# Loading q, k and v of a head pair by one transfer each, with longer rows

## The chip, the cores and the metric

The kernel runs on one core of a Trainium2 chip. The metric is the device time of one execution in microseconds (us), the median of several runs. The core has five engines with instruction streams of their own: PE (TensorE, matrix products; PEld is its loading of weights), DVE (VectorE), ACT (ScalarE), POOL (GpSimd) and SP (SyncE, which here issues nearly all transfers). Sixteen DMA engines move the data of all queues.

## What is computed

Attention over 4 batches of 8 heads, 576 tokens, 64 values a head, then two MoE layers (without routing: plain feed-forward blocks) over all 2304 tokens.

```python
q_d = q.reshape(B, H, S // 4, 4, D).mean(axis=3)          # k_d, v_d alike
out_up = np.repeat(sm_attn(q_d, k_d, v_d), 4, axis=2)      # attention over groups of 4 tokens
mask = np.abs(pos[:, None] - pos[None, :]) < 4             # and over a band of 7 tokens
out_local = masked_attention(q, k, v, mask)
x = (out_up + out_local).transpose(0, 2, 1, 3).reshape(B * S, H * D)     # 2304 x 512
h = x @ w_in;  x = (h * sigmoid(h)) @ w_out                # 512 -> 2048 -> 512
h = x @ w2_in; y = (s * relu(h) ** 2 + b) @ w2_out
```

The MoE weights are stored as 8-byte floats. The kernel makes 4-byte floats of them and splits each into a high and a low part, so that a product takes three matmuls of a faster type.

## The kernel before

The program is a list of operations, each with its engine (or a choice of two), an estimated cost, the buffers that it reads and writes, and a priority (`pr`, lower first). A planner (`Weave.plan`) lays them out: it keeps a clock for each engine, takes the operation that can start first and, among those, the one of lowest `pr`, and so fixes the order of instructions on every engine. For a transfer the cost is a tuple: number of transfers, time on the DMA engines in all, and SP's time for issuing one. Where PE would stand still for long, the planner lays in filling matmuls (`spin`, L369); 100 of them stand at the very start.

Four stages overlap. (1) The first two batches (`NBAND = 2`): for each of four head pairs `rows` loads q, k and v; `b_turn` turns q and k so that the 64 values of a head lie along partitions; `down` does the attention over groups of four tokens; `banded` does the band on PE, with v rows loaded again by `b_load` (`vw`). Their sum goes into `xf`. (2) Batches 2 and 3 load with `natural` and do the band on VectorE (`local`, L480 to L545). (3) The first MoE layer (`mix1`, L835, L855 to L857) runs over five blocks of up to 512 tokens and begins when block 0 of `xf` is done, about 55 us. Its weights (`wi`, `wo`) are loaded and split on VectorE (L379, L382, L385, L391) during batches 0 and 1. (4) From about 390 us the weights of the second layer and then its products.

What matters around the change:

- `rows` (L584): a q or k of a head pair lies in SBUF as 96 partitions x 6 x 128: partition p holds tokens p, 96 + p, 192 + p and so on, with the two heads side by side. It is loaded by two transfers, one a head, whose rows are single tokens of one head, 256 bytes. A v lies as 72 partitions x 2 x 2 x 4 x 64: partition p holds four consecutive tokens, 1024 bytes; two transfers, one for each half of the tokens. The loads of the first batch stand on SP's queue, but for the v of the first pair on ACT's. They take one of ten buffers each (`NNAT`).
- `b_turn` (L702): for q and k, in two halves of 288 tokens, three transposes of 96 x 128 (L716) into one bank of PSUM, then one copy of 128 x 288 to SBUF on ACT or DVE (L333 and L331 on ACT, L335 and L331 on DVE), with the scale for q.
- `pool_rows` (L600) sums v over groups of four; L683 is the product with it. L621 and L622 do the same for the turned q and k.
- Priorities: the loads of a pair are asked for at -2.916 + 0.35 per pair, the first weights at -2.16 and later, and all attention before the weights.

Of the kernel before, what the change touches and what calls it, by code (L numbers as in the profile page):

```python
# [8 lines left out]
F32 = mybir.dt.float32  # L9
# [17 lines left out]
QP = 72  # L27
# [52 lines left out]
class Weave:  # L80
# [9 lines left out]
    def op(self, eng, cost, fn, w=(), r=(), pr=0.0, table=None):  # L90
        n, deps = len(self.ops), set()
        r = [x if isinstance(x, tuple) else (x, None) for x in r]
        w = [x if isinstance(x, tuple) else (x, None) for x in w]

        def hits(d, k):
            return [v for kk, v in d.items() if k is None or kk is None or kk == k]

        for b, k in r:
            deps.update(hits(b.wr, k))
        for b, k in w:  # L100
            deps.update(hits(b.wr, k))
            for v in hits(b.rd, k):
                deps.update(v)
        for b, k in r:
            b.rd.setdefault(k, []).append(n)
        for b, k in w:
            if k is None:
                b.wr, b.rd = {}, {}
            else:
                b.rd.pop(k, None)  # L110
            b.wr[k] = n
        deps.discard(n)
        bufs = []
        for b, _ in r + w:
            if b not in bufs:
                bufs.append(b)
                if not b.left and b.kind in self.turns:
                    self.turns[b.kind].append(b)
                b.left += 1
        self.ops.append((eng if isinstance(eng, tuple) else (eng,), cost, fn, sorted(deps), bufs, pr, table))  # L120
        return n
# [152 lines left out]
def kernel(ctx, tc, q, k, v, w1_in, w1_out, w2_in, w2_out, s2, b2, cst, out):  # L274
    nc = tc.nc
    B, H, S, D = q.shape
# [5 lines left out]
    tens = {"q": q, "k": k, "v": v}  # L282
# [32 lines left out]
    op = W.op  # L315
# [13 lines left out]
    def copy(eng, out, in_, by=1.0):  # L329
        if by == 1.0:  # L330
            (nc.scalar.copy if eng == "act" else nc.vector.tensor_copy)(out=out, in_=in_)  # L331
        elif eng == "act":
            nc.scalar.mul(out=out, in_=in_, mul=by)  # L333
        else:
            nc.vector.tensor_scalar(out=out, in0=in_, scalar1=by, scalar2=None, op0=ALU.mult)  # L335
# [7 lines left out]
    def dma(out, in_, eng=None, **kw):  # L343
        (eng or nc.sync).dma_start(out=out, in_=in_, **kw)  # L344
# [239 lines left out]
    def rows(b, i, names, pr, kind, after=[], by="sp"):  # L584

        for nm in names:
            t = nat[b, i, nm] = Buf(kind, [QP, 2, 2, 4, D] if nm == "v" else [CT, NCT, 2 * D], F32, "n" + nm)

            def load(t=t, nm=nm):
                queue = nc.scalar if by == "act" else nc.sync  # L590
                for k in range(2):
                    row = (b * H + 2 * i) * S
                    if nm == "v":
                        dma(t[:, k].rearrange("p a r d -> p a (r d)"), bass.AP(tens[nm].tensor, (row + k * 4 * QP) * D, [[4 * D, QP], [S * D, 2], [1, 4 * D]]), queue)
                    else:
                        dma(t[:, :, k * D:(k + 1) * D], bass.AP(tens[nm].tensor, (row + k * S) * D, [[D, CT], [CT * D, NCT], [1, D]]), queue)

            op(by, (2, 1.3, 0.4) if nm == "v" else (2, 1.75, 0.8), load, w=[t], r=after, pr=pr)

    def pool_rows(b, i, pr):  # L600

# [11 lines left out]
    def down(b, i, pr, ps="ps"):  # L613
# [66 lines left out]
        for a in range(2):  # L680
            def value(a=a):
                for kt in range(2):
                    nc.tensor.matmul(pU[a * D:(a + 1) * D], lhsT=nat[b, i, "v"][:, kt, a, 0] if plain else sums["v"](kt)[:, a * D:(a + 1) * D],  # L683
                                     rhs=at[:, kt, :, a * DQ:(a + 1) * DQ], start=(kt == 0), stop=(kt == 1))

            op("pe", 0.33 * slow(ps), value, w=[(pU, a), (up, i)], r=[at, nat[b, i, "v"]], pr=pr)
# [15 lines left out]
    def b_turn(b, hq, pr, ps):  # L702

        if hq < 3:
            t = Buf(("lk", "lv", "tmp")[hq], [P, 2, S], F32, "qkT")
            bq[b, hq], bk[b, hq] = (t, 0), (t, 1)
        else:
            bq[b, hq], bk[b, hq] = (Buf("lq", [P, 1, S], F32, "qT"), 0), (Buf("kx", [P, 1, S], F32, "kT"), 0)
        for nm, (t, i) in (("q", bq[b, hq]), ("k", bk[b, hq])):
            r, n = nat[b, hq, nm], S // 2  # L710
            for e in range(2):
                pt = Buf(ps, [P, n], F32, "pq")

                def turn(pt=pt, r=r, e=e):
                    for c in range(NCT // 2):
                        nc.tensor.transpose(pt[:, c * CT:(c + 1) * CT], r[:, e * NCT // 2 + c], ident[:CT, :CT])  # L716

                def keep(eng, pt=pt, t=t, i=i, e=e, nm=nm):
                    copy(eng, t[:, i, e * n:(e + 1) * n], pt[:], -0.125 if nm == "q" else 1.0)

                op("pe", 0.46 * slow(ps), turn, w=[pt, (t, (i, e))], r=[r, csb], pr=pr)
                op(EITHER, (act(n), dve(n)), keep, w=[(t, (i, e))], r=[pt], pr=pr)
# [619 lines left out]
```

## Time and profile before

| | |
|---|---|
| median of 3 runs | 888.25 us (887.92 to 890.25) |
| the profiled execution | 890.97 us, span 889.2 us |
| instructions | 14605 |
| PE, DVE, ACT busy | 867.6, 760.9, 463.8 us |
| transfers | 145.31 MB in 156914 packets; 65452 of them under 512 bytes |

A view's times count from the start of the span. An engine's busy time covers its instructions; a matmul's end is modelled, so a busy PE is not PE at full rate. [...] A DMA share counts the time of all packets against 16 engines and can pass 1, because packets overlap. Idle time at the end of a row is what the engine waited before it, and for whom.

### The profile page before, as it was taken

How to read it: one execution, taken by the hardware profiler on the slowest of the kernel's cores; microseconds unless marked ns; L12 is line 12 of the kernel's file. 1: busy time of each engine (PE TensorE's matmuls, PEld its weight loads, DVE VectorE, ACT ScalarE, POOL GpSimd, SP SyncE). 2: the span in 40 equal slices, each digit the busy share in tenths (PEclk: the TensorE clock that was granted, in tenths of full speed). 3: DMA queues.
4: the chain of work that ended last, by engine and by line, in shares of the span. 5: the costliest groups of instructions: out<-in, count | busy, mean ns of one | idle time of the engine just before them, and what ended most of it. 6: DMA issues, size and time to landing. Idle time of an engine off the chain costs nothing.

```text
span 889.2 us, 14605 instructions
## 1 busy us (share of the span) xinstructions
PE 867.6 (98%) x5303; PEld 716.9 (81%) x5303; DVE 760.9 (86%) x1415; ACT 463.8 (52%) x977; POOL 0.2 (0%) x4
## 2 busy tenths in 40 slices
PE   7999999999999999999999999999999999999998
PEld 7777776777777777878778998888888888888887
DVE  6999999799999999998778868778778768878885
ACT  5965677656457432442215655555657536443442
POOL 0000000000000000000000000000000000000000
PEclk9999999999999999999999999999999999999999
DMA  9999222662524311446988416555668778455511
GB/s 193 261 297 275 78 53 57 151 175 51 126 76 101 125 44 34 142 155 210 302 294 303 140 49 204 185 179 178 208 203 304 265 235 242 141 143 150 135 28 45
DMA packets 156914, 145.31 MB, mean 163 GB/s; under 512 B 65452, under 2 KB 118570, under 8 KB 156842
## 3 DMA queue, kind: packets, MB, share of 16 engines
q1 hardware_dynamic: 156434, 144.01, 54.8%
q8 instruction: 42, 0.69, 0.3%
q10 hardware_dynamic: 408, 0.36, 0.2%
q14 instruction: 30, 0.25, 0.1%
HBM read 103.44 MB, written 40.89 MB: 162 GB/s over the span
## 4 chain that ended last, share of the span: by engine, by line
PE 52%; DVE 28%; DMA 9%; issue 4%; ACT 4%; SPq 3%; DVEq 0%; ACTq 0%
PE ha L835 10%; PE hp L835 10%; PE y L835 6%; PE hc L835 5%; PE oa L1194 4%; DVE tmp L480 4%; DVE sc L483 3%; DVE tmp L517 3%; PE ob L1194 3%; SPq L344 3%; DVE gl L857 3%; PE oc L1194 3%; PE hb L835 2%; PE oa L1195 2%; DMA nq<-in_q_dram 2%
## 5 line engine op out<-in xcount | busy, mean ns | idle before, releaser
L835 PE MATMUL hp<-xh,wi 128*128 128x512 f32 (+1 forms) x640 | 204.0, 381 | 2.9 <-ACT g L855 2.7
L835 PE MATMUL y<-gh,wo 128*128 128x512 f32 (+1 forms) x640 | 200.2, 376 | 0.0
L835 PEld LDWEIGHTS hp<-xh,wi 128*128 128x128 f32 x640 | 117.8, 190 | 28.4 <-ACT g L855 8.3
L835 PEld LDWEIGHTS y<-gh,wo 128*128 128x128 f32 x640 | 117.3, 189 | 20.1 <-issue 1.0
L835 PE MATMUL hp<-xl,wi 128*128 128x512 f32 (+1 forms) x320 | 119.0, 372 | 0.2 <-DVE xl L558 0.2
L835 PE MATMUL y<-gl,wo 128*128 128x512 f32 (+1 forms) x320 | 118.2, 369 | 0.0
L856 ACT CAST gh<-g 128x512 fp32r<-128x512 f32 (+1 forms) x80 | 46.2, 577 | 84.1 <-PE y L835 83.0
L835 PE MATMUL ha<-yh,wi 128*128 128x512 f32 x256 | 87.3, 390 | 0.0
L855 ACT ACTIVATE g<-hp 128x512 f32<-128x512 f32 (+1 forms) x80 | 44.4, 555 | 63.7 <-DVE gl L857 60.1
L835 PEld LDWEIGHTS hp<-xl,wi 128*128 128x128 f32 x320 | 60.9, 190 | 8.4 <-DVE xl L558 0.5
L835 PEld LDWEIGHTS y<-gl,wo 128*128 128x128 f32 x320 | 60.5, 189 | 8.9 <-DVE gl L857 0.4
L835 PEld LDWEIGHTS ha<-yh,wi 128*128 128x128 f32 x256 | 48.1, 188 | 10.0 <-ACT g L331 0.4
L857 DVE TENSOR_TENSOR gl<-g,gh 128x512 fp32r<-128x512 f32 (+1 forms) x80 | 50.4, 630 | 3.7 <-ACT gh L856 3.4
L1033 DVE SCALAR_TENSOR_TENSOR g<-g 128x512 f32<-128x512 f32 (+1 forms) x80 | 48.9, 632 | 3.7 <-ACT g L1032 3.1
L1038 ACT ACTIVATE g<-g,sbt 128x512 f32<-128x512 f32 (+1 forms) x61 | 46.0, 777 | 7.9 <-DVE g L1033 7.6
L835 PE MATMUL ha<-yl,wi 128*128 128x512 f32 x128 | 50.0, 391 | 0.0
L331 ACT COPY g<-ha 128x512 f32<-128x512 f32 x46 | 26.9, 586 | 35.5 <-PE ha L835 23.2
L835 PE MATMUL hc<-yh,wi 128*128 128x512 f32 x128 | 44.8, 389 | 0.0
L1177 DVE TENSOR_TENSOR gl<-graw,gh 128x1024 fp32r<-128x1024 f32 x28 | 33.5, 1218 | 9.0 <-PE oa L1195 5.5
L1194 PE MATMUL oa<-wo,gh 128*128 128x512 f32 x112 | 40.2, 398 | 0.0
L835 PE MATMUL o<-wo,gh 128*128 128x512 f32 x128 | 39.4, 389 | 0.0
L517 DVE TENSOR_TENSOR tmp<-le,lv 128x1344 f32<-128x1344 f32 (+1 forms) x28 | 37.9, 1353 | 0.3
(203 smaller groups left out, 1849.9 us busy)
## 6 DMA issues: line engine op xcount, KB each, us to landing
graw<-gd SPq DMA_DIRECT2D x36, 512.0 KB
gd<-g SPq DMA_DIRECT2D x64, 256.0 KB
wi_raw<-in_moe_w_in_dram SPq DMA_DIRECT2D x16, 512.0 KB
wo_raw<-in_moe_w_out_dram SPq DMA_DIRECT2D x16, 512.0 KB
w_raw<-in_moe_w_in_dram SPq DMA_DIRECT2D x16, 512.0 KB
w_raw<-in_moe_w_out_dram SPq DMA_DIRECT2D x16, 512.0 KB
f<-w2out SPq DMA_DIRECT2D x32, 256.0 KB
nq<-in_q_dram SPq DMA_DIRECT2D x32, 144.0 KB
```

The lines of the kernel that those rows point to most:

```text
L331: (nc.scalar.copy if eng == "act" else nc.vector.tensor_copy)(out=out, in_=in_)
L344: (eng or nc.sync).dma_start(out=out, in_=in_, **kw)
L480: op("dve", dve(n * WIN * D), lambda t=t, i0=i0, n=n, h2=h2: nc.vector.tensor_tensor(out=t[:], in0=wide(qs[:, h2, i0:i0 + n, :].unsqueeze( ...
L517: op("dve", dve(n * WIN * D), lambda t=t, i0=i0, n=n, h2=h2: nc.vector.tensor_tensor(out=t[:], in0=wide(e[:, h2 * ns + i0:h2 * ns + i0 + n ...
L835: nc.tensor.matmul(t(), lhsT=lhs(i), rhs=rhs(i), start=(first and i == 0), stop=(last and i == 2), **kw)
L855: op("act", act(n), lambda g=g, hp=hp: nc.scalar.activation(out=g[:], in_=hp[:], func=AF.Silu), w=[g], r=[hp], pr=-5, table="silu")
L856: op("act", act(n), lambda g=g, gh=gh: nc.scalar.copy(out=gh[:], in_=g[:]), w=[gh], r=[g], pr=-5)
L857: op("dve", dve(n), lambda g=g, gh=gh, gl=gl: nc.vector.tensor_tensor(out=gl[:], in0=g[:], in1=gh[:].bitcast(F32), op=ALU.subtract), w=[gl ...
L1033: op("dve", dve(n) + 1.5 * MORE, lambda: nc.vector.scalar_tensor_tensor(out=t[:], in0=t[:], scalar=0.0, in1=t[:], op0=ALU.max, op1=ALU.mul ...
L1038: nc.scalar.activation(out=t[:], in_=t[:], func=AF.Identity, scale=sbt[:, 0:1], bias=sbt[:, 1:2])
L1177: op("dve", dve(HF * P) + MORE, lambda: nc.vector.tensor_tensor(out=flat(lo), in0=flat(x), in1=flat(hi).bitcast(F32), op=ALU.subtract), w= ...
L1194: nc.tensor.matmul(bank[:].rearrange("p x n -> p (x n)"), lhsT=hi[:, q], rhs=w(), start=new and q == 0, stop=False, skip_group_check=True)
```

## The change

For q and k, partition p now holds three consecutive tokens of each quarter of the pair (two heads, two halves of 288 tokens): 96 x 2 x 2 x 3 x 64, in one transfer with rows of 768 bytes. For v the order of the two middle axes changes (head before half) and both halves come by one transfer with rows of 1024 bytes as before. The heads no longer lie side by side, so each transpose of 96 x 128 becomes two matmuls of 96 x 64 against the same identity matrix, one for each half of the result's partitions. The columns then come out as (c, p) for token 3p + c, so the copy to SBUF puts them in order: it reads PSUM in a row and writes every third element. The planner's costs of the loads change with it. Both batches that use `rows` are affected; `natural` and `local` are not.

```diff
     def rows(b, i, names, pr, kind, after=[], by="sp"):
 
         for nm in names:
-            t = nat[b, i, nm] = Buf(kind, [QP, 2, 2, 4, D] if nm == "v" else [CT, NCT, 2 * D], F32, "n" + nm)
-
-            def load(t=t, nm=nm):
+            t = nat[b, i, nm] = Buf(kind, [QP, 2, 2, 4, D] if nm == "v" else [CT, 2, 2, 3, D], F32, "n" + nm)
+            p, c = (QP, 4) if nm == "v" else (CT, 3)
+
+            def load(t=t, nm=nm, p=p, c=c):
                 queue = nc.scalar if by == "act" else nc.sync
-                for k in range(2):
-                    row = (b * H + 2 * i) * S
-                    if nm == "v":
-                        dma(t[:, k].rearrange("p a r d -> p a (r d)"), bass.AP(tens[nm].tensor, (row + k * 4 * QP) * D, [[4 * D, QP], [S * D, 2], [1, 4 * D]]), queue)
-                    else:
-                        dma(t[:, :, k * D:(k + 1) * D], bass.AP(tens[nm].tensor, (row + k * S) * D, [[D, CT], [CT * D, NCT], [1, D]]), queue)
-
-            op(by, (2, 1.3, 0.4) if nm == "v" else (2, 1.75, 0.8), load, w=[t], r=after, pr=pr)
+                dma(t[:].rearrange("p a e c d -> p (a e) (c d)"), bass.AP(tens[nm].tensor, (b * H + 2 * i) * S * D, [[c * D, p], [p * c * D, 4], [1, c * D]]), queue)
+
+            op(by, (1, 1.3, 0.45) if nm == "v" else (1, 1.2, 0.45), load, w=[t], r=after, pr=pr)
...
-                    nc.tensor.matmul(pU[a * D:(a + 1) * D], lhsT=nat[b, i, "v"][:, kt, a, 0] if plain else sums["v"](kt)[:, a * D:(a + 1) * D],
+                    nc.tensor.matmul(pU[a * D:(a + 1) * D], lhsT=nat[b, i, "v"][:, a, kt, 0] if plain else sums["v"](kt)[:, a * D:(a + 1) * D],
...
                     for c in range(NCT // 2):
-                        nc.tensor.transpose(pt[:, c * CT:(c + 1) * CT], r[:, e * NCT // 2 + c], ident[:CT, :CT])
+                        for a in range(2):
+                            nc.tensor.matmul(pt[a * D:(a + 1) * D, c * CT:(c + 1) * CT], lhsT=r[:, a, e, c], rhs=ident[:CT, :CT], start=True, stop=True)
 
                 def keep(eng, pt=pt, t=t, i=i, e=e, nm=nm):
-                    copy(eng, t[:, i, e * n:(e + 1) * n], pt[:], -0.125 if nm == "q" else 1.0)
+                    copy(eng, t[:, i, e * n:(e + 1) * n].rearrange("d (p c) -> d c p", c=NCT // 2), pt[:].rearrange("d (c p) -> d c p", p=CT), -0.125 if nm == "q" else 1.0)
```

## Rows read from the trace of the kernel before

**Rows 1.** Page: busy time, share of the span and instructions of each engine.
```profile
PE 867.6 (98%) x5303; PEld 716.9 (81%) x5303; DVE 760.9 (86%) x1415; ACT 463.8 (52%) x977; POOL 0.2 (0%) x4
```

**Rows 2.** Windows of stages: PE, PEld, DVE, ACT, POOL busy, clock, DMA share, GB/s.
```profile
0.00:20.00 20.00, 15.17 (x246) 14.01 (x248) 12.06 (x33) 10.27 (x37) 0.20 (x4) 0.91 0.96 200
...
60.00:80.00 20.00, 20.00 (x131) 15.47 (x130) 20.00 (x41) 14.25 (x32) 0.00 (x0) 1.00 1.10 256
...
120.00:140.00 20.00, 19.71 (x178) 14.97 (x179) 19.96 (x52) 14.07 (x41) 0.00 (x0) 1.00 0.22 52
140.00:160.00 20.00, 18.60 (x142) 13.72 (x141) 15.68 (x40) 14.85 (x39) 0.00 (x0) 1.00 0.22 51
160.00:180.00 20.00, 19.85 (x156) 15.06 (x155) 17.53 (x42) 14.20 (x42) 0.00 (x0) 1.00 0.69 167
...
340.00:360.00 20.00, 20.00 (x92) 16.16 (x91) 19.41 (x30) 3.67 (x6) 0.00 (x0) 1.00 0.10 33
```

**Rows 3.** Costliest DVE group, 20 to 140 us: busy us, mean ns, idle before.
```profile
L382 DVE SCALAR_TENSOR_TENSOR f<-wi_raw,f 128x512 int32<-128x512 int32 x16 | 10.9, 682 | 0.0
```

**Rows 4.** DVE in order of time: start, us, instruction, idle before and releaser.
```profile
5.41 0.69 DVE L603 TENSOR_TENSOR nv<-nv 72x512 f32<-72x512 f32 x1 [3.87 <-DMA nv<-in_v_dram]
...
7.50 0.75 DVE L621 TENSOR_REDUCE dq<-qkT 128x144 f32<-128x576 f32 x1 [0.95 <-ACT qkT L333]
...
9.21 0.75 DVE L622 TENSOR_REDUCE dk<-qkT 128x144 f32<-128x576 f32 x1 [0.63 <-ACT qkT L331]
...
11.36 0.46 DVE L335 TENSOR_SCALAR qkT<-pq 128x288 f32<-128x288 f32 x1 [0.47 <-PE pq L716]
...
18.21 0.69 DVE L603 TENSOR_TENSOR nv<-nv 72x512 f32<-72x512 f32 x1 [0.98 <-DMA nv<-in_v_dram]
```

**Rows 5.** The chain that ended last, 0 to 24 us: start, us, what.
```profile
9.64 5.24 DMA nq<-in_q_dram
```

**Rows 6.** A window of one microsecond, columns as in rows 2.
```profile
16.00:17.00 1.00, 1.00 (x16) 0.97 (x15) 1.00 (x4) 0.93 (x5) 0.00 (x0) 0.50 1.00 305
```

**Rows 7.** PE in order of time, columns as in rows 4.
```profile
0.98 4.85 PE L369 MATMUL spin<-idle 128*128 128x64 bf16 x100 [0.98 <-DVE idle L365]
6.28 0.69 PE L716 MATMUL pq<-csb,nq 96*128 96x96 f32 x6 [0.45 <-DMA nq<-in_q_dram]
...
12.80 0.90 PE L651 MATMUL pS<-dk,q_diag 128*96 128x144 f32 x6
15.02 1.09 PE L716 MATMUL pq<-csb,nq 96*128 96x96 f32 x6 [1.32 <-DMA nq<-in_q_dram]
...
21.95 0.72 PE L683 MATMUL pU<-dat,nv 72*64 72x144 f32 x8
```

**Rows 8.** SP's queue in 100:106, 114.4:117.9, 0:10: packets, MB, share of 16 engines.
```profile
q1 hardware_dynamic: 1184, 0.30, 21.5%
q1 hardware_dynamic: 312, 0.30, 27.3%
q1 hardware_dynamic: 5047, 1.35, 81.8%
```

**Rows 9.** SP's issues of the first q, columns as in rows 4.
```profile
1.21 0.97 SPq L344 DMA_DIRECT2D nq<-in_q_dram  x2
```

**Rows 10.** Copies of a turned q: ns least, median, most; first and last start.
```profile
L335 DVE TENSOR_SCALAR qkT<-pq x5: 423/448/456, 11.4 to 115.5; 128x288 f32<-128x288 f32 x5
```

**Rows 11.** Instructions on `upT`, columns as in rows 10: two of 60:175, two of 175:300.
```profile
L825 DVE TENSOR_TENSOR xf<-pBO,upT x11: 348/414/425, 75.5 to 174.3; 128x256 f32<-128x256 f32 x7, 128x192 f32<-128x192 f32 x4
L331 DVE COPY upT<-pU x2: 297/298/300, 136.7 to 153.5; 128x144 f32<-128x144 f32 x2
L542 DVE TENSOR_TENSOR xf<-pt,upT x12: 369/384/417, 226.1 to 257.1; 128x128 f32<-128x128 f32 x12
L331 DVE COPY upT<-pU x1: 301/301/301, 222.0 to 222.0; 128x144 f32<-128x144 f32 x1
```

**Rows 12.** ACT's first table load in 140 to 175 us, columns as in rows 4.
```profile
143.24 1.28 ACT L784 ACT_TABLE_LOAD   x1
```

## The prediction

> **What bounds the kernel now.** I read the page's busy shares first: PE is busy for 98% of the span and VectorE for 86% [rows 1], so little time lies open, and an edit of loads is worth only what a load holds up. The windows of the stages come next [rows 2]. From 0 to 20 us VectorE is busy for only 12.06 us while the DMA engines have a share of 0.96. From 20 us on both are full; the window of 60 to 80 us stands for three (VectorE 20.00 of 20, DMA share 1.10). By 120 to 140 us VectorE is still at 19.96 with a DMA share of 0.22: there the loads hold up nothing. From 340 us on PE alone sets the pace: 92 matmuls, nearly all of the large kind, in 20 us are 0.22 us each. The work that fills VectorE from 20 to 140 us is the making of the MoE weights: for each of 32 tiles three instructions of the length of the group shown, 0.68 us [rows 3], and a shorter one: 32 x 3 x 0.68 = 65 us and more.
>
> Second, VectorE's own order in time from 0 to 20 us [rows 4]. The reader is to see the bracket at the end of a row: 3.87 us idle before the first pooling of v, then 0.95, 0.63, 0.47 and 0.98. In each the bracket's releaser is a load, or a copy or transpose that stands right behind one. Those before 5.41 us are the start (20 - 12.06 = 7.94 us idle in all, of which about 4.7 lie before 5.41); what is left is 3.03 us of named gaps and a few tenths.
>
> Third, the chain that ended last, from 0 to 24 us [rows 5]: the transfer of the first q, SP issuing, the transfer of the third q (5.24 us from 9.64 us), and the transposes behind it. So the first 20 us, and on VectorE they alone, wait for loads. [...]
>
> **What the change does, part by part.**
>
> *Fewer, longer packets for q and k.* A q or k of a head pair is 288 KB, today two transfers of 576 rows of 256 bytes, after it one of 384 rows of 768. Alone on the queues, such a q took 21.5% of 16 engines over 6 us = 20.6 engine-us for 1184 packets, 17.4 ns each; a v of 1024-byte rows took 27.3% of 3.5 us x 16 = 15.3 engine-us for 312 packets, 49 ns each [rows 8]. A packet of 768 bytes lies between; on a straight line it is 17.4 + 31.6 x 512/768 = 38.5 ns (an estimate), so 400 packets (16 end marks among them) cost 15.4 engine-us: 5.2 / 16 = 0.33 us saved a tensor. Under load the 256-byte packets are dearer: in the first 10 us 81.8% of 160 engine-us went to 5047 packets, 25.9 ns each, nearly all of them short [rows 8]. If the long ones rise less, to 46 ns, the saving is (1152 x 25.9 - 400 x 46) / 16 = 0.71 us. I take 0.45 us, nearer to the idle row, since long packets under load must rise too; ends 0.33 and 0.71. Six such tensors come before the second wait for v, so 2.7 us there; eight in the batch, 3.6 us.
>
> *One issue instead of two.* SP needs 0.97 us for the two issues of the first q [rows 9], so with one the first k can be issued 0.97 / 2 = 0.5 us earlier. v keeps its 1024-byte rows; only an issue goes, and its pooling waits for both halves today as well, so the coarser transfer delays nobody.
>
> *Transposes.* Three full-width transposes become six half-width matmuls against the same identity matrix, 32 such groups over both batches. Full width: 0.69 us for six records. Half width with the two halves of the result in different partitions is not there for this size, but the values product has the form: eight records of 72x144 in 0.72 us [rows 7], 0.062 us a record behind a last one of 0.29 us. For 96 columns that scales to 12 x 0.041 + 0.25 = 0.74 us. So +0.05 us a group, and from 20 us on PE has other work in line; I take zero, ends -0.02 (the halves pair perfectly) and +0.5 us a group (they don't pair at all, which the values row speaks against), 16 us over 32 groups. [...]
>
> *Copies out of PSUM.* There are 32 copies, one for each half of a turned q or k; fewer than ten go to VectorE, at 0.45 us [rows 10]. They now write every third element, 12 bytes apart. Lower end: the copies of upT change from unit step in the first batches to a step of two later on, and take 297 to 300 ns and 301 ns on VectorE [rows 11]: nothing. Upper end: the addition that reads PSUM with a step of four takes 384 ns for 128 elements, where one with unit step takes 348 for 192 and 414 for 256 [rows 11]; by these two an element is 66 / 64 = 1.0 ns and 128 would be 282, so the step costs 102 ns for 128, 0.8 ns an element, and 288 elements would pay 0.23 us. For VectorE 9 x 0.23 = 2.1 us over both batches. I take the lower end, since it too is a write, hence zero; the upper stays in the range. [...]
>
> *The planned order.* The cost of a load in the program's own schedule falls from 1.6 to 0.45 us of SP time for a q or k, so every engine's order is laid out anew, on all 890 us. The trace of before can't show that order. What it can do is bounded by the idle time that VectorE has after 20 us: 4.32 us in 140 to 160 us and 2.47 in 160 to 180 [rows 2], where ScalarE loads tables around the last heads of the second batch [rows 12]. A new order can win some of that or lay such a stall in again: -3 to +5 us, 0 taken.
>
> **The sum.** On VectorE: the first gap (0.95) closes only as far as PE is free, since 100 warm-up matmuls hold it to 0.98 + 4.85 = 5.83 us and the first transpose stands at 6.28 [rows 7]: 0.43. The second (0.63) follows the first k, which comes 2 x 0.45 + 0.5 = 1.4 us earlier: all of it. The third (0.47) and fourth (0.98) follow loads that come 1.35 and 2.7 us earlier: all. That is 2.51 us. Behind them ScalarE is next, busy for 10.27 us of the same 20 although it starts late [rows 2], so I give back a fifth: 2.0 us. After 20 us VectorE has no gap to lose, the weights it makes are loaded ahead of it, and 2.0 us earlier there is 2.0 us earlier for x, for PE and for the end. In the second batch nothing is saved: its loads wait for slots that VectorE frees, with a DMA share of 0.22 [rows 2]. The profiled execution took 890.97 us (span 889.2), 2.7 over the median of the runs; 890.97 - 2.0 = 888.97 there, and 888.25 - 2.0 = **886.25** for the median.
>
> **The rivals.** *Reordering costs more than the front gives (slower).* The place is 140 to 175 us, where ScalarE changes between its exp and silu tables six times, 1.28 us each (the first is shown), and VectorE idles most [rows 2, 12]. If heads that are ready earlier are interleaved with one block's silu more finely, each further round is two table loads, 2.57 us, on that chain. One round outweighs the 2.0 us; two give 888.25 - 2.0 + 5.1 = 891.4 us. For it: the order of 890 us hangs on the costs that change. Against it: after 180 us there is other work on every engine. Chance 0.25. *The loads are hidden anyway:* what gates VectorE behind 5.41 us are chains of PE, ScalarE and VectorE, and the gaps move instead of closing: about 888 us, chance 0.09. [...] *More comes off:* with the third q early PE never stands still, the clock stays at 1.00 through 15 to 18 us, and the new order also takes up half of the 6.8 us that VectorE idles in 140 to 180: 888.25 - 2.5 - 3.0 = 882.7 us, chance 0.22. *The halves don't pair on PE:* 16 groups before 55 us mostly hide, the 16 of the second batch cost 8 us: about 894 us, chance 0.03. The forecast itself has 0.35, with 884.5 to 888 as its own range.
>
> **How the numbers follow.** About 0.3%, 2.7 us, is what a measurement can tell from no change here: below 885.6 is faster, above 890.9 slower. Of the forecast's 0.35 some 0.13 lie below 885.6, the rest is the same; with the 0.22 of the larger gain faster is 0.35. Slower takes 0.18 of the 0.25, and the 0.03: 0.21. The rest, 0.44, is the same. The range reaches from the middle of the larger gain to one round and a half of table loads: 882 to 891.5.
>
> **What would show it.** In the profile after: q and k at 768 bytes and some 12,300 packets fewer; the first transpose at about 5.9 us, the third q's before 13 us, no granted clock of 0.5 there; VectorE busy for about 14 of the first 20 us; transposing groups at about 0.7 us and copies at 0.45 us on VectorE. Wrong would be: VectorE's gaps of the first 20 us as long as before (loads hidden), copies of 0.6 us (stride), or a front 2 us earlier with new idle time of VectorE in 20 to 180 us (order). The order of 20 to 180 us is what I know least about.

## The result, and the profile after

The changed kernel takes 898.57 us (median of 5 runs, 894.21 to 899.82) where the kernel before takes 889.4 in the same comparison: a ratio of 1.0088, 95% interval 1.0068 to 1.0107. Run again later it gave 1.0103 (1.0077 to 1.0129). It is slower by about 0.9%, some 8 us; forecast was 886.25 us and a range of 882 to 891.5. The profiled execution took 899.82 us, its span 898.0, so it stands 8.8 us over the profiled execution of before (span 889.2).

The page of the kernel after, in the order PE, PEld, DVE and so on as in [rows 1], and its packets:

```profile
PE 881.3 (98%) x5674; PEld 728.7 (81%) x5674; DVE 765.1 (85%) x1420; ACT 470.1 (52%) x982; POOL 0.2 (0%) x4
...
DMA packets 144277, 145.36 MB, mean 162 GB/s; under 512 B 46668, under 2 KB 105930, under 8 KB 144202
```

There are 12,637 packets fewer, as the change says, and the work of the three busy engines has grown: PE by 13.7 us and 371 instructions (288 for the half-width matmuls, 83 fillers), VectorE by 4.2, ScalarE by 6.3. Windows of the stages, columns as in [rows 2]:

```profile
0.00:20.00 20.00, 16.41 (x284) 15.08 (x285) 9.38 (x20) 10.05 (x30) 0.20 (x4) 0.88 0.95 206
20.00:40.00 20.00, 19.37 (x365) 16.45 (x365) 18.91 (x58) 15.71 (x65) 0.00 (x0) 0.95 1.00 212
...
140.00:160.00 20.00, 19.84 (x182) 14.72 (x181) 19.53 (x49) 15.15 (x47) 0.00 (x0) 1.00 0.27 69
160.00:180.00 20.00, 19.65 (x151) 15.21 (x148) 13.30 (x34) 13.61 (x40) 0.00 (x0) 1.00 0.43 115
```

VectorE is busy for 9.38 of the first 20 us; 14 had been forecast and 12.06 is what before has. What holds it up stands in its own order in time, where the rows that answer to [rows 4] are:

```profile
5.01 0.69 DVE L599 TENSOR_TENSOR nv<-nv 72x512 f32<-72x512 f32 x1 [3.47 <-DMA nv<-in_v_dram]
...
8.28 0.75 DVE L617 TENSOR_REDUCE dq<-qkT 128x144 f32<-128x576 f32 x1 [2.13 <-ACT qkT L333]
...
13.26 0.69 DVE L599 TENSOR_TENSOR nv<-nv 72x512 f32<-72x512 f32 x1 [1.48 <-DMA nv<-in_v_dram]
...
17.49 0.54 DVE L331 COPY qkT<-pq 128x288 f32<-128x288 f32 x1 [0.79 <-PE pq L713]
```

The first gap is 2.13 us instead of 0.95, and the second v holds up what had not waited for it. PE in the same stretch, as in [rows 7]:

```profile
6.43 1.21 PE L713 MATMUL pq<-csb,nq 96*64 96x96 f32 x24 [0.59 <-DMA nq<-in_q_dram]
...
14.70 1.80 PE L713 MATMUL pq<-csb,nq 96*64 96x96 f32 x24 [0.96 <-DMA nq<-in_q_dram]
16.22 2.20 PE L713 MATMUL pq<-csb,nk 96*64 96x96 f32 x24
18.35 1.75 PE L647 MATMUL pS<-dk,q_diag 128*96 128x144 f32 x6
19.89 3.07 PE L369 MATMUL spin<-idle 128*128 128x64 bf16 x67
...
23.80 0.61 PE L805 MATMUL pBT<-csb,be 128*72 128x128 f32 x4
```

The reader is to see three things. A turned q takes 1.21 us, not 0.69. The third q's group starts at 14.70 us, hardly before the 15.02 of [rows 7], although its transfer starts at 5.00 us instead of 9.64 [rows 5]: it takes 9.56 us, not 5.24. And the turning of the first head's weights (`pBT`) stands behind the third q and k, a score product and a long filler, at 23.80 us; in before it is at 16.62. The transfer in the chain that ended last, as in [rows 5]:

```profile
5.00 9.56 DMA nq<-in_q_dram
```

The granted clock is told as a share of PE's full clock. In before it is 0.50 at 16 to 17 us [rows 6], where the six records of the third q take 1.09 us, against 0.69 us for those of the first [rows 7]. In after PE was at half clock for longer, after it had stood still for 1.3 us of 13 to 15 us, and the third q's group takes 1.80 us against 1.21:

```profile
13.00:14.00 1.00, 0.40 (x5) 0.25 (x5) 0.71 (x2) 0.00 (x0) 0.00 (x0) 1.00 1.13 247
14.00:15.00 1.00, 0.30 (x7) 0.33 (x9) 1.00 (x4) 0.00 (x0) 0.00 (x0) 1.00 1.06 225
15.00:16.00 1.00, 1.00 (x21) 1.00 (x18) 1.00 (x3) 0.43 (x1) 0.00 (x0) 0.58 0.85 172
...
21.00:22.00 1.00, 1.00 (x24) 1.00 (x22) 1.00 (x5) 0.43 (x3) 0.00 (x0) 0.51 1.01 211
```

### The profile page after: what moved, and what is told of

Read it like the earlier page. It is cut to its first block, busy times and chain, and to the rows that moved or that the text cites. A ratio compares the mean times of both kernels' runs of the same rounds, so it can differ in the third digit from the quotient of the medians.

```text
span 898.0 us, 15328 instructions
## 1 busy us (share of the span) xinstructions
PE 881.3 (98%) x5674; PEld 728.7 (81%) x5674; DVE 765.1 (85%) x1420; ACT 470.1 (52%) x982; POOL 0.2 (0%) x4
## 4 chain that ended last, share of the span: by engine, by line
PE 60%; DVE 27%; DMA 7%; issue 3%; ACT 2%; SPq 0%; DVEq 0%; ACTq 0%
PE hp L832 11%; PE ha L832 10%; PE y L832 9%; PE hc L832 5%; PE oa L1191 4%; DVE tmp L517 3%; DVE tmp L480 3%; PE ob L1191 3%; PE oc L1191 3%; DVE sc L483 3%; DVE gl L854 3%; PE hb L832 2%; PE oa L1192 2%; DVE tmp L522 2%; PE o L832 2%
## 5 line engine op out<-in xcount | busy, mean ns | idle before, releaser
L832 PE MATMUL hp<-xh,wi 128*128 128x512 f32 (+1 forms) x640 | 201.8, 378 | 1.7 <-ACT g L852 1.4
```

What stands on the lines that cost most here:

```text
L832: nc.tensor.matmul(t(), lhsT=lhs(i), rhs=rhs(i), start=(first and i == 0), stop=(last and i == 2), **kw)
```

## The experiments

The change has four parts: the loads, the half-width matmuls, the copies with a step of three, and the planner's costs, which lay out all engines anew. Each was run alone or left out. The table has all runs. The ratio is of medians; the columns behind it are read from one profiled execution of each run: its time, VectorE's busy time and the GB/s from 0 to 20 us, the start of the first y (the first product with `wo` on PE, which opens the second half of the MoE's first block), and PE's busy time from 66 us to the end.

| run | ratio to before (95%) | profiled, us | VectorE busy, 0 to 20 us | GB/s, 0 to 20 us | first y, us | PE busy from 66 us |
|---|---|---|---|---|---|---|
| before |  | 890.97 | 12.06 | 200 | 66.46 | 809.07 |
| step of three alone | 0.9999 (0.9979 to 1.0019) | 889.22 | 12.17 | 198 | 66.95 | 807.78 |
| half width alone | 1.0036 (1.0015 to 1.0056) | 891.44 | 12.32 | 199 | 66.30 | 812.52 |
| loads alone | 0.9999 (0.9984 to 1.0015) | 886.50 | 14.15 | 226 | 64.62 | 805.50 |
| loads alone, again | 0.9983 (0.9967 to 0.9999) | 889.76 | 13.59 | 224 | 65.43 | 806.32 |
| loads, half width in first batch | 1.0009 (0.9993 to 1.0025) | 889.29 | 13.29 | 212 | 65.86 | 806.66 |
| loads, half width in second batch | 1.0017 (1.0001 to 1.0032) | 891.81 | 13.33 | 213 | 65.24 | 811.91 |
| all operations of after, old order | 1.0048 (1.0027 to 1.0070) | 890.54 | 11.74 | 208 | 67.95 | 812.66 |
| small step of one cost, old operations | 0.9989 (0.9973 to 1.0005) | 887.56 | 12.16 | 196 | 66.27 | 807.00 |
| new order alone | 1.0063 (1.0039 to 1.0088) | 893.85 | 11.90 | 209 | 70.55 | 811.84 |
| new order alone, short fillers | 1.0060 (1.0035 to 1.0084) | 894.35 | 10.10 | 193 | 73.59 | 813.71 |
| new order, old costs for first loads | 1.0030 (1.0012 to 1.0049) | 889.00 | 11.70 | 188 | 65.77 | 808.11 |
| new costs for first loads only | 1.0088 (1.0058 to 1.0117) | 895.95 | 11.35 | 203 | 73.97 | 813.79 |
| all but half width | 1.0046 (1.0031 to 1.0061) | 888.83 | 13.37 | 228 | 68.19 | 808.63 |
| after | 1.0088 (1.0068 to 1.0107) | 899.82 | 9.38 | 206 | 73.92 | 820.22 |
| after, again | 1.0103 (1.0077 to 1.0129) | 901.65 | 8.69 | 209 | 74.25 | 820.41 |
| after, costs fitted to landings | 1.0172 (1.0139 to 1.0205) | 906.12 | 8.84 | 206 | 75.38 | 823.18 |

A profiled execution need not be a typical one. That of "new order, old costs for first loads" took 889.00 us where the median of the run is 892.34, that of "all but half width" 888.83 against 893.76.

**Operations against order.** First the two halves of the question: everything but the order, and the order alone.

```diff
 # all operations of after, old order
-            op(by, (1, 1.3, 0.45) if nm == "v" else (1, 1.2, 0.45), load, ...)
+            op(by, (2, 1.3, 0.4) if nm == "v" else (2, 1.75, 0.8), load, ...)
```

> The changed kernel with the planner's costs of before, so that every engine's order is that of the kernel before and only the operations differ (long rows, one issue, half-width matmuls, copies with a step of three). Theory A, the order: the changed kernel lost its 9 us because loads planned as cheap laid the order out anew; then this one is near the kernel before, 887 to 891 us. Theory B, the operations: a group of transposes costs PE 0.67 us instead of 0.41 (32 groups, 8 us in all) and a copy costs ScalarE 0.15 us more (25 copies, 3.8 us); then it stays slow, 895 to 899 us. Both in halves: about 893 us.

> The kernel before with the planner's costs of the changed one: the operations of before in the order of the changed kernel. Theory A, the order: 895 to 899 us, with VectorE idle for some 4 us in 160 to 180 us again. Theory B, the operations: 888 to 891 us.

The second is the kernel before with the costs of the line marked with a minus. Both lose: 0.48% and 0.63%. So part of the loss is in what the instructions do, and somewhat more in where they stand; the two add up to 1.11%, a little over the 0.88% and 1.03% of after.

**The order.** The row that shows it is where the first y starts, and the product `hp` that must come before it. PE's groups of 20 to 66 us (busy us, mean ns, idle before), of before, of the new order alone and of after:

```profile
L835 PE MATMUL hp<-xh,wi 128*128 128x512 f32 x39 | 14.0, 409 | 0.6 <-ACT g L855 0.6
L369 PE MATMUL spin<-idle 128*128 128x64 bf16 x257 | 9.9, 193 | 0.0
L835 PE MATMUL hp<-xl,wi 128*128 128x512 f32 x19 | 7.6, 398 | 0.2 <-DVE xl L558 0.2
```

```profile
L369 PE MATMUL spin<-idle 128*128 128x64 bf16 x311 | 12.0, 194 | 0.0
L835 PE MATMUL hp<-xh,wi 128*128 128x512 f32 x28 | 10.8, 419 | 0.0
L835 PE MATMUL hp<-xl,wi 128*128 128x512 f32 x14 | 5.5, 392 | 0.0
```

```profile
L369 PE MATMUL spin<-idle 128*128 128x64 bf16 x386 | 15.4, 198 | 0.6 <-issue 0.6
L832 PE MATMUL hp<-xh,wi 128*128 128x512 f32 x21 | 8.5, 427 | 0.0
L832 PE MATMUL hp<-xl,wi 128*128 128x512 f32 x10 | 3.9, 393 | 0.0
```

By 66 us PE has done 58 matmuls of `hp` in before (21.6 us), 42 with the new order (16.3 us, 5.3 less) and 31 in after (12.4 us, 9.2 less); the whole is slower by 5.6 us (0.63%) and by 7.8 to 9.2. PE is busy all the same, with fillers and, in after, with half-width matmuls in their place. What is left for it then, for the same three (the first figure behind the comma is PE's busy time):

```profile
66.00:889.20 823.20, 809.07 (x4411) 667.29 (x4409) 703.12 (x1268) 416.26 (x813) 0.00 (x0) 1.00 0.52 156
```

```profile
66.00:892.10 826.10, 811.84 (x4427) 670.17 (x4425) 706.86 (x1272) 423.60 (x829) 0.00 (x0) 1.00 0.51 156
```

```profile
66.00:898.00 832.00, 820.22 (x4583) 676.36 (x4581) 711.09 (x1277) 426.27 (x831) 0.00 (x0) 1.00 0.51 155
```

From 66 us on PE stands still for only 14.1 of 823 us in before and for 10 to 16 us in every run, so what it has not done by then comes on top. With the new order alone 2.8 us more are left (less than the 5.3 of `hp`, since other work had gone ahead), and that execution's span is 2.9 us longer: there the loss is made before 66 us. By the medians the new order alone loses 5.6 us; what makes up the rest no profile shows. In after 11.2 us more are left, 4 to 5 of them for half-width groups that come behind 66 us, and the span is 8.8 us longer, with 2.3 us less of idle time. Across the table the first y says the same: the profiled executions with a y behind 70 us took 893.85 us and more, the others 886.50 to 891.81.

How the order makes it late can be followed in ScalarE and PE, though no run changes this place alone. The planner now believes that loads land sooner, so it puts PE's work on the second q and k ahead of the first band scores (`pB`, at 11.73 instead of 8.98 us), that on the third k ahead of the first turned weights, and ScalarE's copies of the third q ahead of the first exps. In the kernel before the first exp on ScalarE and the turned weights on PE:

```profile
11.41 0.34 ACT L784 ACTIVATE be<-be,bst 128x72 f32<-128x72 f32 x1
...
16.62 1.05 PE L808 MATMUL pBT<-csb,be 128*72 128x128 f32 x4
```

and with the new order alone, where the first exp stands behind a copy that waited 1.77 us for PE:

```profile
14.55 0.71 ACT L333 ACTIVATE qkT<-pq 128x288 f32<-128x288 f32 x2 [1.77 <-PE pq L716]
15.29 0.35 ACT L784 ACTIVATE be<-be,bst 128x72 f32<-128x72 f32 x1
...
16.30 2.35 PE L369 MATMUL spin<-idle 128*128 128x64 bf16 x75
19.76 0.60 PE L808 MATMUL pBT<-csb,be 128*72 128x128 f32 x4 [1.11 <-ACT de L655]
```

Five runs put this to the test. Does any new layout cost something; does the layout lose because it expects loads too early; does the place of the first three pairs carry it; do the long fillers? (The edits are shortened.)

```diff
 # small step of one cost, old operations
-... else (2, 1.75, 0.8), load
+... else (2, 1.75, 0.7), load
 # after, costs fitted to landings
-op(by, (1, 1.3, 0.45) if nm == "v" else (1, 1.2, 0.45), load
+op(by, (1, 2.6, 0.45) if nm == "v" else (1, 1.45, 0.45), load
 # new order, old costs for first loads (and, with the two swapped, new costs for first loads only)
+op(by, (old) if b == 0 and i < 3 else (new), load
 # new order alone, short fillers
-self.fill(int((begin[i] - now) * FILLD / 0.03))
+self.fill(min(FILLN, int((begin[i] - now) * FILLD / 0.03)))
```

> The kernel before with one number changed: a load of q or k counts 0.7 instead of 0.8 us of SP's time in the planner. No instruction is added or taken away; the planned order of all engines comes out anew (some 1300 of VectorE's instructions stand elsewhere). If the order of after loses because its numbers say that loads land earlier than they do, this small step costs nothing: 888 to 891 us where before is at 889.3. If any new order loses, because the costs of before give an unusually good one, it costs 2 to 6 us: 891.5 to 895.5.

> The kernel after, with the planner told when its loads land by the profile after: 2.6 us behind the issue for v and 1.45 for q and k, instead of 1.3 and 1.2. Instructions are those of after, only the order differs. If the order of after loses because it expects the loads too early, this gains most of the 5.5 us back: 893 us or less where before is at 889.3 (the half-width matmuls stay). If any new order loses about as much, it stays at 896 to 900 us.

> The operations of before in the order that the planner makes with the costs of after, except that the loads of the first three head pairs of the first batch keep their old costs; so VectorE's, ScalarE's and PE's order in the first 20 us is that of before, and behind it everything is laid out anew. Theory of the front: the new order loses its 0.6% because PE takes up the second k and third q ahead of the first band scores, so the first exps on ScalarE (11.41 us in before, 15.29 in the run with the new order alone) and the first turned weights (16.62 against 19.76 us) come 3 to 4 us late, and the rest follows 3 us late. Then this run is back within 0.2% of before, 888 to 891 us where before is at 889.3. Theory of the rest: the new order loses in 100 to 180 us or in the stage behind 700 us; then it stays at 893.5 to 896.

> The other way round: the operations of before, the new costs for the loads of the first three head pairs alone, the old ones for the other five. Theory of the front: the first exps come at 15 us again and the whole loses 0.4 to 0.7%, 893 to 895.5 us where before is at 889.3. Theory of the rest: 888 to 891. If both this run and the one with old costs for the first loads lose, each new layout costs something and no single place does.

> The operations of before in the order of after, but a filler of PE (matmuls that keep it busy where the plan leaves a gap) has at most 14 matmuls: the group of 75 behind the third head pair's score product, 2.35 us, shrinks to 14, and the other long ones with it; no other instruction moves. If the filler holds up the turned weights behind it, this wins 1.5 to 2.5 us back: 892 to 893.5 where before is at 889.3 and the new order alone at 895. If it doesn't (PE stood still for 1.11 us behind it, waiting for ScalarE), it stays at 894 to 896.

The small step costs nothing (0.9989), so a new layout as such is not dear. Costs nearer to the landings lose still more (1.0172), which speaks against "it expects the loads too early": a truer number does not give a better order here. The front carries most of it: new costs for the first three pairs alone lose 0.88%, old costs for them leave 0.30%. But the two don't add up to the 0.63% of both together, so by what was written before no single place holds it all. Where the 0.30% lie is not shown: the profiled execution of that run, at 889.00 us, has neither a late y nor more work left at 66 us. The fillers are not shown to be it either: with 14 instead of 75 PE waits longer in front of `pBT` for the same ScalarE, and the ratio stays.

```profile
18.24 0.57 PE L369 MATMUL spin<-idle 128*128 128x64 bf16 x14
21.68 0.60 PE L808 MATMUL pBT<-csb,be 128*72 128x128 f32 x4 [2.87 <-ACT de L655]
```

But with the fillers the granted clock went too. It is 0.83 from 20 to 40 us, where the new order with its long fillers has 1.00, and this may have taken back what the shorter fillers won:

```profile
20.00:40.00 20.00, 16.85 (x229) 13.69 (x231) 17.48 (x55) 14.92 (x63) 0.00 (x0) 0.83 1.01 210
```

**The half-width matmuls.**

```diff
-                        nc.tensor.transpose(pt[:, c * CT:(c + 1) * CT], r[:, e * NCT // 2 + c], ident[:CT, :CT])
+                        for a in range(2):
+                            nc.tensor.matmul(pt[a * D:(a + 1) * D, c * CT:(c + 1) * CT], lhsT=r[:, e * NCT // 2 + c, a * D:(a + 1) * D], rhs=ident[:CT, :CT], ...)
```

> The kernel before, loads and order unchanged, with each transpose of 96x128 made by two half-width matmuls. Theory B: PE pays 0.26 us more for each of 32 groups, those of the first batch on the way to the first scores and those of the second on a full PE, so 892 to 896 us; the granted clock may fall in the first 20 us as PE's groups stretch. Theory A, or the forecast of this document that the halves cost nothing: 888 to 890 us.

Alone they cost 0.36%, 3.2 us. The granted clock did not fall: it is 1.00 in the first 20 us. One group that stands by itself, of before and of after:

```profile
26.19 0.41 PE L716 MATMUL pq<-csb,nq 96*128 96x96 f32 x3
```

```profile
25.95 0.72 PE L713 MATMUL pq<-csb,nq 96*64 96x96 f32 x12
```

A transpose is one record (one entry of the trace), a half-width matmul is two; a group goes from 3 records to 12 and from 0.41 to 0.72 us, 0.31 us more; two groups that follow each other go from 0.69 to 1.21, 0.26 us more each. Over 32 groups that is 8 to 10 us of PE, of which 3.2 us came through. The trace says where. The first y is not late (66.30 us, in before 66.46), the last `pBO` of the second batch is, by 3.1 us; in before and with half width alone:

```profile
173.56 0.69 PE L817 MATMUL pBO<-bat,vw 72*64 72x64 f32 x16
```

```profile
176.69 0.69 PE L818 MATMUL pBO<-bat,vw 72*64 72x64 f32 x16
```

So by these profiles the 16 groups of the first batch are covered by time in which PE stood still or filled, and the 16 of the second are mostly paid. Undone in the order of after, and put into one batch each on top of the loads:

> The kernel after with one part undone: the transposes are again three full-width transposes a group, each on 128 neighbouring columns of a loaded tensor. These columns hold other tokens and heads than the ones wanted, so the turned q and k are mixed up; the amount of work, the loads of 768 bytes, the copies with a step of three and the order of after are kept. If the parts add up as the first four runs have them (after 1.0088 of before, half-width matmuls alone 1.0036), this one stands at 1.005 to 1.006 of before, some 894 us in a call where before is at 889.3, and its groups take 0.41 us and six records again. If the half-width matmuls cost nothing in the order of after, because PE waits there anyway, it stays at 1.008 to 1.009, 897 us. If they are the whole loss in that order, it is within 0.2% of before.

> The loads alone in the old order (768 bytes a row, unit-step copies, q and k mixed up), and the half-width matmuls in the first batch only; the second batch keeps full-width transposes. So far three kernels with both long rows and half-width matmuls moved 206 to 208 GB/s in the first 20 us and three with long rows and full-width transposes 224 to 228, and the third q's transposes began at 14.7 to 18.3 against 12.3 to 12.6 us. If the half-width matmuls of the first 20 us slow the loads down, this run shows 206 to 208 GB/s, the third q after 14.5 us, VectorE below 12.5 us of 20, and loses 1.5 to 2.5 us against the loads alone. If the loss of the half-width matmuls lies in the second batch, as 8 us of PE that nothing hides, this run stays within 1 us of the loads alone: 888 to 890 where before is at 889.3.

> The complement: half-width matmuls in the second batch only, loads, order and the rest as in the other. If half-width matmuls in the first 20 us slow the loads, this one keeps 224 to 228 GB/s there, the third q before 13 us and VectorE at 13.5 us or more. If it is the mere presence of longer code, or where things come to lie in memory, it falls to 206 to 208 as well, since no half-width matmul runs before 100 us. In time: 891 to 893 us where before is at 889.3 if the second batch carries the loss (16 groups at 0.27 us, 4.3 us of PE, most of it in the open), 888 to 890 if the first batch does.

Without them the kernel after stands at 1.0046, 0.42% to 0.57% below its own 1.0088 and 1.0103, so they cost about the same in either order. Of the batches, over the 0.9991 that is the mean of the two runs of the loads alone, the first costs 0.18% and the second 0.26%; the intervals overlap, so only the profiles speak for the second. The last `pBO` of the second batch, of the loads alone (again), of half width in the first batch and in the second:

```profile
172.30 0.69 PE L814 MATMUL pBO<-bat,vw 72*64 72x64 f32 x16
```

```profile
173.33 0.69 PE L818 MATMUL pBO<-bat,vw 72*64 72x64 f32 x16
```

```profile
175.68 0.69 PE L818 MATMUL pBO<-bat,vw 72*64 72x64 f32 x16
```

1.0 us late against 3.4, where the two executions of the loads alone lie 0.8 us apart.

**The step of three.**

```diff
-                    copy(eng, t[:, i, e * n:(e + 1) * n], pt[:], ...)
+                    copy(eng, t[:, i, e * n:(e + 1) * n].rearrange("d (p c) -> d c p", c=NCT // 2), pt[:].rearrange("d (c p) -> d c p", p=CT), ...)
```

> The kernel before, with only the copies of the turned q and k writing every third element; the tokens of a half then lie in another order, which leaves out the right order of the tokens and no work. The changed kernel's profile has 0.55 us a copy on ScalarE instead of 0.40 and 0.54 instead of 0.45 on VectorE: 23 x 0.15 + 9 x 0.09 = 4.3 us in all, mostly on ScalarE, which is not full. Theory B: 889 to 892 us, 1 to 3 us over the kernel before on the way to the first scores. Theory A: no change, 888 to 890 us.

No change of time (0.9999, to 0.2% either way). Yet each copy is longer, in the groups of after (count, busy us, mean ns):

```profile
L331 ACT COPY qkT<-pq 128x288 f32<-128x288 f32 x10 | 5.2, 548 | 1.2 <-PE pq L713 1.1
L335 DVE TENSOR_SCALAR qkT<-pq 128x288 f32<-128x288 f32 x4 | 2.2, 544 | 1.1 <-PE pq L713 1.0
```

On VectorE 544 ns against the 448 of [rows 10], 0.1 us more for 288 elements; on ScalarE 548 against 393 in before; the run with the step alone has 555 to 562 ns on ScalarE. Some 32 copies by 0.10 to 0.15 us are hidden.

**The loads.** To have them without the half-width matmuls, the full-width transposes take 128 neighbouring columns of the new layout, the copies go in a row, and the order is that of before.

```diff
+                        x = r[:].rearrange("p a e c d -> p (a e c d)")
+                        nc.tensor.transpose(pt[:, c * CT:(c + 1) * CT], x[:, (e * NCT // 2 + c) * P:(e * NCT // 2 + c + 1) * P], ident[:CT, :CT])
```

> The loads of after alone: 768 and 1024 bytes a row and one transfer a tensor, with full-width transposes on 128 neighbouring columns (so the turned q and k are mixed up, the amount of work is that of before), unit-step copies, and the planner's old costs, so that every engine keeps the order of before. The prediction's theory: the loads land earlier and VectorE's gaps of the first 20 us close, VectorE is busy for about 14 of them and the whole is 2 us shorter, 887.3 where before is at 889.3. The theory from the profile after: the transfers move bytes at the same rate with long rows as with short ones (206 against 200 GB/s in the first 20 us), the first q and k land where they did, VectorE stays at 12 of 20 us, and the whole is within 1.5 us of before. Third: v on 72 partitions loads only part of the DMA engines and holds up what is queued behind it; then VectorE has less than 11.7 us of the first 20 and the whole is 1 to 2 us longer.

> The run with the loads alone in the old order once more, with more rounds (q and k mixed up as there). Its profile showed the gain that was predicted, VectorE busy for 14.15 of the first 20 us and every later instruction 2.0 to 2.5 us earlier, yet the median showed no gain (0.9999). If that profile was of an unusual execution, in which PE kept its full clock in the first 20 us, another execution shows a granted clock below 1.00 there, VectorE below 13 us, and the median stays within 0.15% of before. If the gain is real and the first interval fell at its end, the median is 1.5 to 2.5 us below before, a ratio of 0.997 to 0.9985.

In both profiles the front is what was forecast. The window of the second, and its third q:

```profile
0.00:20.00 20.00, 16.18 (x268) 14.79 (x269) 13.59 (x38) 10.82 (x40) 0.20 (x4) 0.91 0.95 224
...
12.63 0.69 PE L713 MATMUL pq<-csb,nq 96*128 96x96 f32 x6 [0.83 <-DMA nq<-in_q_dram]
```

The first y is 1.84 and 1.03 us earlier. At the end little is left: 0.9999 and 0.9983, 0.8 us in the mean, and zero is not excluded. In the profile of the second run one sees where a lead of 1.3 us goes: VectorE's first sum of the next batch's q waits for its transfer, where in before (175.23 us) it did not wait.

```profile
175.22 0.69 DVE L605 TENSOR_TENSOR nq<-nq 72x512 f32<-72x512 f32 x1 [1.16 <-DMA nq<-in_q_dram]
```

The first of the two profiles kept its lead past there (173.20 us). So this is one way to lose it, not shown to be the rule.

**After once more.**

> The kernel after itself once more, for a tighter ratio and a second profile. If its loads are slower than those of the runs with full-width transposes for good, it shows 203 to 210 GB/s in the first 20 us again, the third q after 14 us and VectorE at 8.5 to 10.5 us; if the first profile was of an unusual execution, 220 GB/s or more and the third q before 13 us. The ratio to before stays at 1.007 to 1.010; the sum of the parts measured singly is 1.0063 (order) times 1.0036 (half-width) times 0.999 (loads), 1.009.

The first profile was no exception: 209 GB/s, VectorE 8.69 us, the third q's group at 15.54 us. The parts measured singly give 1.0063 x 1.0036 x 0.9999 x 0.9991 = 1.0089; after gave 1.0088 and 1.0103.

## Why the prediction was wrong, step by step

The forecast had the kernel 2.0 us faster, and it is 7.8 us slower, 9.8 us apart. Three terms make that up: the order (0 taken, 5.6 measured), the half-width matmuls (0 taken, 3.2 measured) and the earlier front (2.0 taken, 0.8 measured): 5.6 + 3.2 + 1.2 = 10.0.

*What bounds the kernel.* The reading of [rows 1] and [rows 2] was too quick on PE. Its 98% include 403 fillers, 17.0 us of the 867.6, all of them before 66 us (257 in the group above, 146 in the first 20 us); "busy" there does not mean at its work. Behind 66 us it is the other way: PE is busy for 809.07 of 823.20 us and sets the pace, not only from 340 us on, where the prediction says "PE alone" and its own row has VectorE at 19.41 of 20. The prediction followed VectorE's gaps; what counts is how much PE has left at 66 us.

*Transposes* is the step that failed in size: zero was taken, 3.2 us came (1.3 to 5.0 by the interval). It read the six records of 0.69 us in [rows 7] as one group and found 0.05 us of difference to 0.74. The code has three transposes a group, so that row holds two groups; one alone is 0.41 us. The forecast of the new group (0.74 against 0.72 measured) was right, that of the old one was not. Counted by record the old form shows nothing to lose: a transpose takes 0.09 us for 96 columns and the score product 0.12 us for 144, about the same per column [rows 7]. But that product takes two records for each matmul, and a transpose one, so there was a factor of two to lose. The traces show one record for a transpose and two for a half-width matmul (3 a group against 12); the full-width score product has two as well, and no run here has a half-width transpose, so why a transpose takes only one is not shown. The cover that the step named ("PE has other work in line") was there for the first batch and not for the second, where PE is busy for 18.60 to 20.00 of 20 us in the windows of [rows 2]. The rival *the halves don't pair* had this place right ("mostly hide", then paid) and 0.03 of the chance; its mechanism was not it, since the new group costs what the forecast said.

*The planned order* failed in place. Zero was taken with -3 to +5 us, for a stall at 140 to 175 us around more rounds of table loads. The cost is 5.6 us (3.5 to 7.8), and in the profiled execution of the new order alone (2.9 us longer than that of before) it is made before 66 us, as PE's work put off. The place that was priced doesn't show it: from 140 to 180 us VectorE stands still for 6.0 us with the new order alone, 7.2 in after and 6.8 in before. Table loads are 40 in both, and from 140 to 175 us there are three in after (the next stands at 175.08) instead of the six of before, whose first is in [rows 12]:

```profile
141.32 1.28 ACT L852 ACT_TABLE_LOAD   x1
151.24 1.28 ACT L651 ACT_TABLE_LOAD   x1
160.81 1.28 ACT L852 ACT_TABLE_LOAD   x1
```

The rival *reordering costs more* was right in sign (891.4 us) and wrong in mechanism.

*Fewer, longer packets* was right as a mechanism, and its size depends on the program. SP's queue in the first 10 us, of after and of the loads alone, as in [rows 8]:

```profile
q1 hardware_dynamic: 2167, 1.53, 78.4%
```

```profile
q1 hardware_dynamic: 2338, 1.70, 75.2%
```

Per MB that is 82 and 71 engine-us, against 97 in before (81.8% of 160 for 1.35 MB). Other transfers are mixed into these. For the 0.295 MB of a q it saves 0.28 us in after, under the lower end, and 0.48 with the loads alone; 0.45 had been taken, with ends 0.33 and 0.71. *One issue instead of two* was right: the first q is issued in 0.42 us instead of 0.97.

*The sum* is right up to 20 us where the loads stand alone (14.15 and 13.59 us of VectorE's work, about 14 forecast) and falls where it says that 2.0 us there are 2.0 us at the end: 0.8 were found, with zero within reach; the rival *hidden anyway* (0.09) comes nearest to that.

*Copies* was right in time (nothing) and wrong in the instruction: zero was taken, 0.10 us on VectorE came, below the upper end of 0.23 (which had 0.06 of the chance, at 888.35 us); the longer copies of ScalarE, which does most of them, were not looked at. On VectorE steps of 12 bytes do cost here (544 against 448 ns), where steps of 8 showed nothing in [rows 11] (301 against 297 to 300 ns).

*The clock.* "No granted clock of 0.5" was wrong: after has it from about 15.2 to 22 us, behind the stretch from 13 to 15 us in which PE stood still for 1.3 us, most of it for a third q that lands at 14.56 us. The sum had no term for this, and the rival *more comes off* counted on the opposite, an early third q and a clock that stays at 1.00. The mean granted clock of every execution is on record, and the time goes with it: the eleven executions of after took 894.2 and 894.7 us at 1.000 and 0.999, 896.6 to 899.0 at 0.998 and 898.8 to 901.7 at 0.996, where before has medians of 889.0 at 1.000 (45 executions) and 890.3 at 0.996 (11). So at full clock, by two executions, the loss is some 5 us, and 3 to 4 us more go with the half clock. Whether it makes them or comes along with a late third q, no run separates. The four kinds of new order on old operations that lose (new order alone, short fillers, old and new costs for the first loads) never ran above 0.998, so a part of what is booked here to the order may be clock.

Open remain: why the same transfers move 206 to 209 GB/s in the four profiles with all half-width matmuls, 212 and 213 with half of them, and 224 to 228 in the three without. It begins before the first of these matmuls runs (251 and 265 GB/s from 3 to 6 us in after and with the loads alone), and also where they run only in the second batch (there from 66 us on, not only behind 100 us as was expected), so they don't do it by running. Open is also what makes one order better than another, beyond the late first exps.

## What to carry to other kernels

Where a planner fixes the order, a changed cost is a change to the whole program: price it by how much the engine that sets the pace has left when its dense work begins, and count fillers out of its busy time first. Before taking a row as the price of one operation, hold its count of records against the code. Work added to the engine that sets the pace is paid where that engine has neither idle time nor fillers to take it up: of 8 to 10 us added here 3.2 came through, by the profiles mostly in the second batch. And a lead won at the loads in front may be given back at the next load.

## What the runs showed of the hardware

A transpose of 96 x 128 in fp32 is one record on PE, and the same by two half-width matmuls is four: 0.41 against 0.72 us a group of three. Rows three times as long (768 instead of 256 bytes) moved 3 to 14% more bytes in the first 20 us (206 to 228 against 200 GB/s), not a multiple. A transfer that starts 4.6 us earlier while the DMA engines are full (share 1.06 to 1.13 from 13 to 15 us) lands 0.3 us earlier: the third q, at 14.56 us in after and 14.88 in before [rows 5]. And the same kernel's executions differ in the first 20 us, by PE's clock among others: the loads alone were profiled with 1.00 and with 0.91 there, and its front lay 0.8 us apart at the first y.
